# A first layer's weights finished by an accumulating DMA, and one output of the first token pair by seven products

## The chip, the cores and the metric

The kernel runs on one core of one Trainium2 chip. The metric is device microseconds (us) of one execution, the median over runs; a profile of one further execution gives the trace. PE is TensorE (matmuls), PEld its weight loads, DVE is VectorE, ACT is ScalarE, POOL is GpSimd and SP is SyncE, which here only issues DMAs.

## The reference

An attention over 256 channels, then two feed-forward layers of 2048 hidden columns, on 6016 tokens. The weights come in as float64.

```
qn = q / (norm(q, axis=1) + 1e-6);  kn = k / (norm(k, axis=1) + 1e-6)
a = softmax(kn.T @ qn / tau)              # 256 x 256, summed over 6016 tokens
x = v @ a                                 # 6016 x 256
h = x @ w_in;  g = h * sigmoid(1.702 * h) # 2048 columns
x = g @ w_out
h = x @ w_in2; g = max(h, 0) + alpha * min(h, 0)
out = g @ w_out2
```

## The kernel before, in words

**Numbers.** Every operand is kept as two float32r halves, hi and lo, and a product is three matmuls: hi by hi, hi by lo, lo by hi (`PASSES`). A matmul of the bulk is 128x128 weights by 512 tokens.

**Stages.** First q and k stream in and PE builds the 256 x 256 matrix of their products (gram, L348); ACT and DVE build the norms; a softmax follows (L457 to L480). The attention matrix is multiplied into the first layer's inner weights, so that v goes straight into the feed-forward layer: `emit_w(j)` (L483) makes the inner weights of output block j, `emit_pair(j)` (L628) of two blocks at once. Then come twelve token columns in six pairs, for layer 0 and then for layer 1; j counts eight blocks (`NQ`) of 256 hidden columns.

**The first pair.** For layer 0 the first pair of columns is run by `direct` while its weights are still being made. One unit of `direct` is one half block by one column: two products into one PSUM bank (L684), with the output products of the block before (`outs.next()`, L713) between them, 12 matmuls in all. Then, for the unit, ACT writes g (L761) and its hi half (L775), `mid_way` may emit weights, `beside(FIRST)` fills in background work, and DVE writes the lo half (L781). There are four units to a block, i = 0 to 3. All other pairs are run by `quartet`, which needs seven products instead of eight for a block and column pair (sums of operands, `T1` to `T4`, and sums of weights, `combine_wi`, prepared by DVE and ACT).

**The converter.** Float64 weights are turned into hi and lo by `Convert`, a piece of 512 columns (or 1024) at a time. Its steps: `load` (SP, into the buffer `raw`), `scale` (ACT, L130), `shift` (DVE, L133), `signed` (DVE, L137), `copy` (ACT, L143, the hi half), `power` (DVE, L147), `rest` (DVE, L150), `less` (DVE, L166) and `low` (DVE, L169, the lo half). `conv.todo` is the list of pieces: ia[j] for inner, ob_[j] for outer weights. `Converter.step` does the next DVE step; ACT's parts go onto the list `put_off`, which `beside` empties first. `beside` also takes steps while its time allows, and `need` takes them until a piece is made. So the order on every engine is fixed when the program is built; each engine runs its own list in order, and waits on semaphores for the others. `raw` has two buffers, and `rest` is the last step that reads one: the next load waits for it.

Of the kernel before, what the change touches and what calls it, by code (L numbers as in the profile page):

```python
# [15 lines left out]
P = 128  # L16
N = 6016
C = 256
# [16 lines left out]
TAIL = 12  # L35
ON_VECTOR = (4, 5, 6, 8)
# [20 lines left out]
def attention_then_two_ffns(ctx: ExitStack, tc: tile.TileContext, q, k, vT, tau, w1i, w1o, w2i, w2o, alpha, outT):  # L57
# [45 lines left out]
    class Convert:  # L103
# [4 lines left out]
        most = 2 * PIECE  # L108
        pool = None

        def __init__(self, src, pair, done=None):
            self.src, self.pair, self.done = src, pair, done
            self.made = False
            self.a = src.shape[1]
            self.n = self.a * src.shape[2]
# [7 lines left out]
        def load(self):  # L123
            self.raw = self.tile("raw", U32, RAWS, 2)
            nc.sync.dma_start(self.raw.rearrange("p (a n) w -> p a (n w)", a=self.a), u32(self.src))

        def scale(self):

            self.p = self.tile("p", F32, 2)
            nc.scalar.activation(self.p, f32(self.raw[:, :, 1]), AF.Copy, scale=2.0**-112)  # L130
# [4 lines left out]
        def signed(self):  # L135
            self.top = self.tile("top", F32, 1)
            nc.vector.scalar_tensor_tensor(u32(self.top), self.raw[:, :, 1], 0x80000000, u32(self.p),  # L137
                                           ALU.bitwise_and, ALU.bitwise_or)
            self.hi, self.lo = self.pair()
            put_off.append(self.copy)  # L140

        def copy(self):
            nc.scalar.copy(self.hi, self.like(self.top))  # L143
# [30 lines left out]
    class Converter:  # L174


        STEPS = (("shift", 0.45), ("signed", 0.7), ("power", 0.45), ("rest", 0.7), ("less", 0.7), ("low", 0.7))

        def __init__(self):
            self.todo, self.loaded, self.ready, self.open, self.at = [], [], [], None, 0  # L180

            self.ahead = False
            self.held = 0

        def load(self):

            while self.todo and len(self.loaded) + len(self.ready) + self.held < RAWS:
                x = self.todo.pop(0)
                x.load()
                self.loaded.append(x)  # L190

        def scale(self):
            if self.loaded and not self.ready:
                x = self.loaded.pop(0)
                put_off.append(x.scale)
                self.ready.append(x)

        def cost(self):
            return self.time(self.open or (self.ready + self.loaded + self.todo)[0])

        def time(self, piece):
            t = self.STEPS[self.at][1]
            return 2 * t - 0.15 if piece.n > PIECE else t

        def waits(self):

            if not self.open:
                if not self.loaded and not self.ready:
                    self.load()
                self.scale()  # L210
            return any(x in put_off for x in self.needs())

        def needs(self):
            return [self.ready[0].scale] if self.at == 0 else [self.open.copy] if self.at == 4 else []

        def step(self):

            if self.waits():
                scalar_work()
            if not self.open:  # L220
                self.open = self.ready.pop(0)
                self.held = 1
            do, t = self.STEPS[self.at][0], self.time(self.open)
# [7 lines left out]
            if self.at == len(self.STEPS):  # L231
                self.open, self.at = None, 0
            return t
# [5 lines left out]
        def need(self, pieces):  # L239
            while not all(x.made for x in pieces):  # L240
                self.step()

        def left(self):
            return self.todo + self.loaded + self.ready + [x for x in (self.open,) if x]
# [10 lines left out]
    with tc.manual_schedule():  # L255
# [15 lines left out]
        def inner(j, n=1):  # L271
            def pair():
                if j % 2 == 0:
                    t = wi_whole[j] = wi_first.pop() if wi_first else wi_tiles()
                    for i in range(2):
                        wi_pair[j + i] = tuple(x[:, :, i * C:(i + 1) * C] for x in t)
                    if n == 2:
                        return [flat(x) for x in t]
                return wi_pair[j]
            return Convert(w1i.rearrange("p (a n) -> p a n", a=2)[:, :, j * C:(j + n) * C], pair)  # L280

        def outer(j, n=1):
            def pair():
                return tuple(WO[:, j:j + n, h].rearrange("p q a b -> p q (a b)") if n > 1 else flat(WO[:, j, h]) for h in range(2))
            return Convert(w1o[:, j * PIECE:(j + n) * PIECE].rearrange("p (a n) -> p a n", a=1), pair)

        ia, ob_ = {}, {}
        for made, piece, spans in ((ia, inner, ((0, 1), (1, 1), (2, 1), (3, 1), (4, 2), (6, 2))),
                                   (ob_, outer, ((0, 1), (1, 1), (2, 1), (3, 1), (4, 2), (6, 2)))):
# [254 lines left out]
        def prepare(l, p):  # L544
# [4 lines left out]
            ops = operands[l, p] = {}  # L549
# [40 lines left out]
            ]  # L590
            return early, late
# [63 lines left out]
        def beside(time, convert=False, place=None, most=None):  # L655

            now = scalar_work(most)
# [19 lines left out]
        def finish(steps):  # L677

            while any(s in bg for s in steps):
                bg.pop(0).run()  # L680
# [102 lines left out]
        def direct(j, outs, mid_way):  # L783

            ops = operands[0, 0]
            units = []
            for i, (f, c) in enumerate((f, c) for f in range(2) for c in range(2)):
                ps = begun.pop(0) if begun else None
                for h in range(2):
                    if h == 0 and ps:  # L790
                        continue
                    ps = ps or psh.tile([P, T], F32, tag="h", name="ps_h")
                    product(ps, j, 2 * h + f, ops[h, c], T, h == 0, h == 1)
                    outs and outs.next()
                u = Unit(0, 2 * j + f, c)
                u.take(ps)
                u.act()
                u.high()
                mid_way(i)
                beside(FIRST, convert=True)  # L800
                u.low()
                units.append((f, c, u.pair))
            return Outs(0, 0, j, units)

        def quartet(l, p, j, outs, carry):
# [3 lines left out]
            late = steps_late if j == 0 else []  # L809

# [3 lines left out]
            def copy(ps):  # L814
                s = sp.tile([P, T], F32, tag="s", name="s", bufs=3)
# [5 lines left out]
            most = 1 if l else None  # L821
# [105 lines left out]
        del raws[0, 0], raws[0, 1]  # L927
        outs = None
        steps_late = []
        combined = []  # L930
        for j in range(NQ):
# [3 lines left out]
            def mid_way(i):  # L935
                if j == 0 and i == 1:
                    conv.need([ob_[0]])
                    emit_w(1)
                if j in (1, 2, 3, 5) and i == 1:
                    (emit_w if j < 3 else emit_pair)(j + 1)  # L940
                if j == 2 and i == 0:
                    nc.sync.dma_start(alpha_sb, alpha)
                if j == 3 and i < 2:
                    load_tokens(0, 2 + i)
                if j == 5 and i == 0:
                    early, late = prepare(0, 1)
                    bg.extend(early + late)
                    for n in range(AHEAD):
                        combined.append(combine_wi(n))
                        bg.extend(combined[n])  # L950

            outs = direct(j, outs, mid_way)
        conv.need(ob_.values())
        finish(list(bg))
# [4 lines left out]
        stage = stx.enter_context(tc.tile_pool(name="stage", bufs=3, side="right"))  # L959
        Convert.pool, Convert.most = stx.enter_context(tc.tile_pool(name="cn", bufs=1, side="right")), PIECE  # L960
# [40 lines left out]
        carry = []  # L1001
        order = [(0, p) for p in range(1, NP)] + [(1, p) for p in range(NP)]
        for i, (l, p) in enumerate(order):
# [6 lines left out]
            for j in range(NQ):  # L1010
# [18 lines left out]
                if i == 0 and j + AHEAD < NQ:  # L1029
                    combined.append(combine_wi(j + AHEAD))  # L1030
                    first(combined[-1])
# [12 lines left out]
                if i == 0 and j + 1 < NQ:  # L1044
# [56 lines left out]
```

## Time and profile before

| | |
|---|---|
| median of 3 runs | 1034.63 us (1034.33 to 1034.76) |
| the profiled execution | 1034.38 us |
| its span, first to last instruction | 1032.6 us |
| PE busy | 1027.4 us (99%), 4640 matmul records |
| DVE busy | 765.3 us (74%) |
| ACT busy | 752.8 us (73%) |
| POOL busy | 31.3 us (3%) |

The busy shares are averages over the whole span. A matmul record of the bulk lasts 385 ns, but matmuls are pipelined and overlap, so the time that one adds is read from the starts of a run of them. Idle time before an instruction stands in brackets in a timeline, with what ended it.

### The profile page before, as it was taken

What the parts mean: (1) busy time and instruction counts of PE and PEld (TensorE: products, weight loads), DVE (VectorE), ACT (ScalarE), POOL (GpSimd) and SP (SyncE); (2) the same over time, 40 slices, a digit from 0 to 9 for tenths busy, and PEclk for the clock granted to TensorE, in tenths of its full rate; (3) what the DMA queues carried; (4) which work ended last, traced back from release to release, by engine and by line L of the source; (5) the groups of instructions that cost most, each with busy time, mean ns of one, the idle gap of its engine ahead of it and who ended that gap; (6) DMA issues with size and microseconds to landing.
All of it is one profiled execution on the core that took longest, in us unless ns stands there. A gap on an engine that the chain in (4) does not pass through costs nothing.

```text
span 1032.6 us, 12486 instructions
## 1 busy us (share of the span) xinstructions
PE 1027.4 (99%) x4640; PEld 866.8 (84%) x4640; DVE 765.3 (74%) x1230; ACT 752.8 (73%) x1255; POOL 31.3 (3%) x42
## 2 busy tenths in 40 slices
PE   9999999999999999999999999999999999999998
PEld 8888888888888888888998888888888888888997
DVE  4889967878778787445637777787877787877766
ACT  6777767778777777666767777777777777867776
POOL 4400000000000000000100000000000000000000
PEclk9999999999999999999999999999999999999999
DMA  9635102125224323003543001001001000000101
GB/s 361 240 106 180 42 23 95 42 77 179 77 82 158 101 93 133 1 1 126 200 169 113 1 21 62 1 21 62 1 21 62 1 18 25 35 0 1 42 1 36
DMA packets 30461, 77.62 MB, mean 75 GB/s; under 512 B 3008, under 2 KB 7616, under 8 KB 30144
## 3 DMA queue, kind: packets, MB, share of 16 engines
q1 hardware_dynamic: 28096, 65.29, 18.2%
q0 software_dynamic: 2304, 11.54, 3.4%
q8 instruction: 36, 0.59, 0.2%
q14 instruction: 25, 0.20, 0.1%
HBM read 52.96 MB, written 23.86 MB: 74 GB/s over the span
## 4 chain that ended last, share of the span: by engine, by line
PE 99%; DMA 0%; SPq 0%; ACT 0%; issue 0%
PE ps_o L713 50%; PE ps_h L684 44%; PE gram L348 4%; PE pw L483 1%; PE pw L628 1%; DMA qk<-in_k 0%; SPq L368 0%; PE nrm L426 0%; ACT s L730 0%; PE bc L448 0%; PE pt L471 0%
## 5 line engine op out<-in xcount | busy, mean ns | idle before, releaser
L713 PE MATMUL ps_o<-ghi,wo 128*128 128x512 f32 (+1 forms) x1536 | 561.6, 385 | 0.0
L684 PE MATMUL ps_h<-x,wi 128*128 128x512 f32 (+1 forms) x2040 | 550.5, 385 | 0.0
L684 PEld LDWEIGHTS ps_h<-x,wi 128*128 128x128 f32 x2040 | 382.2, 188 | 72.4 <-DVE wi L495 0.4
L713 PEld LDWEIGHTS ps_o<-ghi,wo 128*128 128x128 f32 x1536 | 288.3, 188 | 53.5
L713 PE MATMUL ps_o<-glo,wo 128*128 128x512 f32 (+1 forms) x768 | 296.0, 385 | 0.0
L750 DVE TENSOR_TENSOR g<-ps_h,s 128x512 f32<-128x512 f32 (+1 forms) x177 | 120.0, 678 | 94.1 <-PE ps_h L684 60.4
L779 DVE SCALAR_TENSOR_TENSOR glo<-g,sign_sb,ghi 128x512 fp32r<-128x512 f32 (+1 forms) x192 | 141.4, 736 | 55.5 <-ACT ghi L773 51.1
L816 ACT COPY s<-ps_h 128x512 f32<-128x512 f32 (+1 forms) x177 | 102.2, 577 | 104.7 <-PE ps_h L684 100.4
L781 DVE TENSOR_TENSOR glo<-g,ghi 128x512 fp32r<-128x512 f32 (+1 forms) x192 | 126.4, 677 | 68.1 <-ACT ghi L775 67.9
L713 PEld LDWEIGHTS ps_o<-glo,wo 128*128 128x128 f32 x768 | 144.2, 188 | 27.3 <-DVE glo L779 0.3
L773 ACT ACTIVATE ghi<-g,sign_sb 128x512 fp32r<-128x512 f32 (+1 forms) x192 | 137.0, 714 | 16.1 <-DVE g L769 10.8
L775 ACT CAST ghi<-g 128x512 fp32r<-128x512 f32 (+1 forms) x192 | 113.3, 612 | 3.6
L761 ACT ACTIVATE g<-ps_h 128x512 f32<-128x512 f32 (+1 forms) x112 | 65.7, 587 | 44.6 <-PE ps_h L684 43.9
L765 ACT ACTIVATE g<-g,sign_sb 128x512 f32<-128x512 f32 (+1 forms) x97 | 69.5, 717 | 29.2 <-DVE g L750 28.6
L769 DVE SCALAR_TENSOR_TENSOR g<-g,slope_sb 128x512 f32<-128x512 f32 (+1 forms) x97 | 71.6, 738 | 16.8 <-ACT g L765 16.6
L769 DVE SCALAR_TENSOR_TENSOR g<-ps_h,slope_sb,g 128x512 f32<-128x512 f32 (+1 forms) x95 | 69.7, 733 | 0.0
L827 ACT COPY ps_h<-ps_h 128x512 f32<-128x512 f32 (+1 forms) x87 | 49.0, 563 | 28.2 <-PE ps_h L684 27.6
L765 ACT ACTIVATE g<-ps_h,sign_sb 128x512 f32<-128x512 f32 (+1 forms) x95 | 64.3, 676 | 2.2 <-ACT g L765 0.3
L761 ACT ACTIVATE g<-g 128x512 f32<-128x512 f32 (+1 forms) x80 | 49.8, 623 | 15.5 <-DVE g L750 15.3
L348 PE MATMUL gram<-qk 128*128 128x256 f32 x156 | 34.3, 380 | 0.3 <-DMA qk<-in_k 0.3
L348 PEld LDWEIGHTS gram<-qk 128*128 128x128 f32 x156 | 29.4, 190 | 4.6 <-issue 0.7
L563 DVE TENSOR_TENSOR x<-t,x 128x512 fp32r<-128x512 f32 (+1 forms) x44 | 29.0, 671 | 0.0
(115 smaller groups left out, 498.6 us busy)
## 6 DMA issues: line engine op xcount, KB each, us to landing
wi<-w2i POOLq DMA_DIRECT2D x8, 896.0 KB, 4.9
xraw<-in_vT SPq DMA_DIRECT2D x10, 512.0 KB, 6.1
x<-ob SPq DMA_DIRECT2D x20, 256.0 KB, 2.3
xraw<-x SPq DMA_DIRECT2D x10, 512.0 KB, 3.5
out_T<-ob SPq DMA_DIRECT2D x20, 256.0 KB, 2.1
qk<-in_q SPq DMA_DIRECT2D x9, 512.0 KB, 10.2
qk<-in_k SPq DMA_DIRECT2D x9, 512.0 KB, 10.3
raw<-in_w2i SPq DMA_DIRECT2D x8, 512.0 KB, 4.2
```

The costliest lines, as they stand in the source:

```text
L348: nc.tensor.matmul(gram[m][:, :C], tiles[i][:, 1, r, m * P:(m + 1) * P], tiles[i][:, 0, r, :], start=(t == 0), stop=(t == R - 1))
L684: nc.tensor.matmul(ps[:, :n], WI[:, wq, a, blk], x[:, b, :n], start=(start and i == 0), stop=(stop and i == 2), skip_group_check=True)
L713: nc.tensor.matmul(acc_ps[c][d][:, :n], WO[:, j, a, f, d * P:(d + 1) * P], (hi, lo)[b][:, :n], start=(start and i == 0), stop=(stop and i ...
L750: nc.vector.tensor_tensor(self.src, ps[:, :self.n], s[:, :self.n], ALU.add)
L761: nc.scalar.activation(self.g, self.src, AF.Gelu_apprx_sigmoid)
L765: nc.scalar.activation(self.g, self.src, AF.Copy, scale=sign_sb[:, self.f])
L769: nc.vector.scalar_tensor_tensor(self.g, self.src, slope_sb[:, self.f], self.g, ALU.mult, ALU.max)
L773: nc.scalar.activation(self.hi, self.g, AF.Copy, scale=sign_sb[:, self.f])
L775: nc.scalar.copy(self.hi, self.g)
L779: nc.vector.scalar_tensor_tensor(self.lo, self.g, sign_sb[:, self.f], f32(self.hi), ALU.mult, ALU.subtract)
L781: nc.vector.tensor_tensor(self.lo, self.g, f32(self.hi), ALU.subtract)
L816: nc.scalar.copy(s[:, :n], ps[:, :n])
```

## The change

1. **An accumulating DMA.** Pieces ia[3] to ia[7] and ob_[2] to ob_[7] are `added`: after `rest`, POOL issues a DMA that adds `top` onto `p` (`sent`), ACT copies `p` to the hi half, and one DVE subtraction (`split`) gives the lo half; `less` and `low` go. All pieces are 512 wide now; there are three `raw` buffers, five of `p` and three of `top`.
2. **Given out by places.** Each call of `beside` is a place (`conv.place`). A piece's `scale` is put off until `LOADING` = 2 places after its load was issued, its copy until `LANDING` = 3 places after the DMA was issued, unless `need` asks for it.
3. **Seven products.** Block 7 of the first pair goes through `quartet`; its operand sums are prepared from block 4 on, the weight sums of block 7 from block 5 on.
4. **Buffers.** Five of the eleven token buffers lie in the lower pool instead of four.

```
+LOADING = 2
+LANDING = 3
+STRASSEN = 7
...
-            self.raw = self.tile("raw", U32, RAWS, 2)
+            self.begun = conv.now
+            self.raw = self.tile("raw", U32, Convert.raws, 2)
...
+        def sent(self):
+            self.begun = conv.now
+            nc.gpsimd.dma_start(out=self.p, in_=self.top, accum_op=ALU.add)
+
+        def split(self):
+            nc.vector.tensor_tensor(self.lo, self.like(self.p), f32(self.hi), ALU.subtract)
+            self.made = True
...
+        ADDED = (("shift", 0.45), ("signed", 0.7), ("power", 0.45), ("rest", 0.7))
...
-        def scale(self):
-            if self.loaded and not self.ready:
+        def scale(self, force=False):
+            while self.loaded and not self.ready and (force or not (self.ahead and Convert.deep) or self.now - self.loaded[0].begun >= LOADING):
                 x = self.loaded.pop(0)
                 put_off.append(x.scale)
                 self.ready.append(x)
...
+        def ask(self):
+            if self.flying and not self.flying[0].asked:
+                self.flying[0].asked = True
+                put_off.append(self.flying[0].copy)
...
+        def place(self):
+            self.now += 1
+            if self.ahead and Convert.deep:
+                self.scale()
+                if self.flying and self.now - self.flying[0].begun >= LANDING:
+                    self.ask()
...
-        conv.todo = [ia[1], ob_[0], ia[2], ob_[1], ia[3], ob_[2], ia[4], ob_[3], ob_[4], ia[6], ob_[6]]
+        conv.todo = [ia[1], ob_[0], ia[2], ob_[1], ia[3], ob_[2], ia[4], ia[5], ob_[3], ob_[4], ia[6], ia[7], ob_[5], ob_[6], ob_[7]]
...
-            return xin[i > 3].tile([P, 2, T], F32R, tag=f"x{i}", name="x")
+            if slot[0] <= 8:
+                i = (2, 1, 4, 0, 3, 5, 6, 7)[i]
+            return xin[i > 4].tile([P, 2, T], F32R, tag=f"x{i}", name="x")
...
         def beside(time, convert=False, place=None, most=None):
 
+            conv.place()
             now = scalar_work(most)
...
+                if j == 4 and i == 0:
+                    sums0.extend(prepare(0, 0))
+                    bg.extend(sums0)
...
+            if j < STRASSEN:
+                outs = direct(j, outs, mid_way)
+                continue
...
+            outs = quartet(0, 0, j, outs, carry)
```

The change moves instructions on ACT and DVE around `emit_w(3)`, which PE runs right after unit i = 1 of block 2. On ACT, before, from unit i = 1 of block 1 to unit i = 3; wi_hi_563<-top_626 is the hi half of ia[3], `p<-raw` a `scale`:

```order
L761 ACTIVATE g_647<-ps_h_630 128x512
L775 CAST ghi_645<-g_647 128x512
L491 ACTIVATE wi_436<-pw_650,rs_127 128x256 x2
L143 CAST wi_hi_563<-top_626 128x2x256
L761 ACTIVATE g_689<-ps_h_674 128x512
L775 CAST ghi_687<-g_689 128x512
L130 ACTIVATE p_692<-raw_598 128x512
L761 ACTIVATE g_714<-ps_h_699 128x512
L775 CAST ghi_712<-g_714 128x512
```

With the change, from the two weight rows of that piece (L571, before L491) to the copy of ia[3] behind unit i = 0 of block 2; p_599 is the sum of ia[3], raw_572 holds ob_[2], raw_603 ia[4], raw_673 ia[5] and raw_702 ob_[3]:

```order
L571 ACTIVATE wi_438<-pw_653,rs_127 128x256 x2
L137 ACTIVATE p_670<-raw_572 128x512
L848 ACTIVATE g_695<-ps_h_680 128x512
L862 CAST ghi_693<-g_695 128x512
L137 ACTIVATE p_698<-raw_603 128x512
L848 ACTIVATE g_724<-ps_h_709 128x512
L862 CAST ghi_722<-g_724 128x512
L137 ACTIVATE p_727<-raw_673 128x512
L848 ACTIVATE g_751<-ps_h_736 128x512
L862 CAST ghi_749<-g_751 128x512
L137 ACTIVATE p_755<-raw_702 128x512
L154 CAST wi_hi_568<-p_599 128x2x256
```

The hi half of ia[3] moved from before unit i = 2 of block 1 to behind unit i = 0 of block 2, and behind the scales of ob_[2], ia[4], ia[5] and ob_[3].

On DVE, before, from `rest` of ia[3] to `rest` of ob_[2]; the third row is the lo half of ia[3]:

```order
L150 SCALAR_TENSOR_TENSOR p_622<-raw_567,p_622 128x512
L166 TENSOR_TENSOR top_626<-top_626,wi_hi_563 128x512
L169 TENSOR_TENSOR wi_lo_564<-top_626,p_622 128x2x256
L781 TENSOR_TENSOR glo_646<-g_647,ghi_645 128x512
L133 TENSOR_SCALAR p_692<-p_692 128x512
L137 SCALAR_TENSOR_TENSOR top_695<-raw_598,p_692 128x512
L147 TENSOR_SCALAR p_692<-top_695 128x512
L781 TENSOR_TENSOR glo_688<-g_689,ghi_687 128x512
L150 SCALAR_TENSOR_TENSOR p_692<-raw_598,p_692 128x512
```

With the change, from `signed` of ob_[2] on (`rest` of ia[3] and `shift` of ob_[2] stand right ahead of it) to the lo half of ia[3], the last row:

```order
L144 SCALAR_TENSOR_TENSOR top_677<-raw_572,p_670 128x512
L868 TENSOR_TENSOR glo_649<-g_650,ghi_648 128x512
L158 TENSOR_SCALAR p_670<-top_677 128x512
L161 SCALAR_TENSOR_TENSOR p_670<-raw_572,p_670 128x512
L140 TENSOR_SCALAR p_698<-p_698 128x512
L144 SCALAR_TENSOR_TENSOR top_706<-raw_603,p_698 128x512
L868 TENSOR_TENSOR glo_694<-g_695,ghi_693 128x512
L158 TENSOR_SCALAR p_698<-top_706 128x512
L161 SCALAR_TENSOR_TENSOR p_698<-raw_603,p_698 128x512
L140 TENSOR_SCALAR p_727<-p_727 128x512
L868 TENSOR_TENSOR glo_723<-g_724,ghi_722 128x512
L168 TENSOR_TENSOR wi_lo_569<-p_599,wi_hi_568 128x2x256
```

The lo half of ia[3] moved behind the four steps of ob_[2], the four of ia[4] and the first of ia[5]. Ahead of `rest` of ia[3] DVE's list is as before back to the gram's end.

On SP, in the change, the loads from ia[4] to ob_[4], behind which alpha's follows:

```order
L132 DMA raw_603<-in_w1i 128x2x512
L132 DMA raw_673<-in_w1i 128x2x512
L132 DMA raw_702<-in_w1o 128x1024
L132 DMA raw_731<-in_w1o 128x1024
L1048 DMA alpha_sb_69<-in_alpha 128x16
```

The load of ia[5] (raw_673) takes the buffer that `rest` of ia[3] frees, that of ob_[3] (raw_702) the one that `rest` of ob_[2] frees. In the first loads behind q and k, ob_[0] now stands ahead of the two loads of tokens, and ia[2] ahead of tau.

## Rows read from the trace of the kernel before

**Rows 1.** The page, parts 1, 2 and 4: busy time, clock in 40 slices, chain.
```profile
PE 1027.4 (99%) x4640; PEld 866.8 (84%) x4640; DVE 765.3 (74%) x1230; ACT 752.8 (73%) x1255; POOL 31.3 (3%) x42
...
PEclk9999999999999999999999999999999999999999
...
PE 99%; DMA 0%; SPq 0%; ACT 0%; issue 0%
```

**Rows 2.** Waits of PE over the whole span: total us, times, longest.
```profile
PE idle L308 <- POOL ones L301: 1.1, 1, 1.1
PE gram L348 <- DMA qk<-in_k: 0.3, 1, 0.3
```

**Rows 3.** The chain in order of time: start, us, what.
```profile
147.13 1.36 PE ps_o L713 x6
```

**Rows 4.** Stretches: length, then busy us of PE, PEld, DVE, ACT, POOL; clock, DMA, GB/s.
```profile
77.10:91.00 13.90, 13.90 (x63) 11.49 (x62) 13.12 (x19) 10.11 (x18) 0.00 (x0) 1.00 0.37 115
...
133.50:146.50 13.00, 13.00 (x59) 10.75 (x58) 7.00 (x16) 6.74 (x12) 0.00 (x0) 1.00 0.00 1
```

**Rows 5.** Timeline of PE at `emit_w(3)`: start, us, what.
```profile
75.42 0.40 PE L483 MATMUL pw<-wi_hi,eT_hi 128*128 128x256 f32 x2
75.66 0.40 PE L483 MATMUL pw<-wi_lo,eT_hi 128*128 128x256 f32 x2
```

**Rows 6.** Timeline of DVE, from `rest` of ia[3] on.
```profile
70.39 0.68 DVE L150 SCALAR_TENSOR_TENSOR p<-raw,p 128x512 f32<-128x512 uint32 x1
71.00 0.68 DVE L166 TENSOR_TENSOR top<-top,wi_hi 128x512 f32<-128x512 f32 x1
71.71 0.69 DVE L169 TENSOR_TENSOR wi_lo<-top,p 128x512 fp32r<-128x512 f32 x1
...
72.92 0.42 DVE L133 TENSOR_SCALAR p<-p 128x512 uint32<-128x512 uint32 x1
...
75.05 0.68 DVE L150 SCALAR_TENSOR_TENSOR p<-raw,p 128x512 f32<-128x512 uint32 x1
```

**Rows 7.** Timeline of SP: issues of tau and of a load of weights.
```profile
35.32 0.34 SPq L417 DMA_DIRECT2D tau_sb<-in_tau  x1
...
71.15 0.55 SPq L125 DMA_DIRECT2D raw<-in_w1i  x1
```

**Rows 8.** DMA issues from 60 to 72 us: count, KB each, us to landing.
```profile
raw<-in_w1i SPq DMA_DIRECT2D x1, 512.0 KB, 4.0
raw<-in_w1o SPq DMA_DIRECT2D x1, 512.0 KB, 3.5
```

**Rows 9.** Timeline of ACT around the same place.
```profile
65.17 0.66 ACT L130 ACTIVATE p<-raw 128x512 f32<-128x512 f32 x1
65.74 0.59 ACT L761 ACTIVATE g<-ps_h 128x512 f32<-128x512 f32 x1
...
66.89 0.47 ACT L491 ACTIVATE wi<-pw,rs 128x256 fp32r<-128x256 f32 x1
...
69.86 0.61 ACT L143 CAST wi_hi<-top 128x512 fp32r<-128x512 f32 x1
...
76.47 1.15 ACT L130 ACTIVATE p<-raw 128x1024 f32<-128x1024 f32 x1 [0.59 <-DMA raw<-in_w1i]
```

**Rows 10.** DMA issues of line L1037, POOL's loads of weights of 896 KB each.
```profile
DMA to landing us min/median/max: 4.7/4.9/6.8
```

**Rows 11.** Timeline of ACT at the end of the gram.
```profile
39.44 0.62 ACT L325 CAST x<-xraw 128x512 fp32r<-128x512 f32 x1
41.79 0.37 ACT L429 COPY G<-gram 128x256 f32<-128x256 f32 x1 [1.74 <-PE gram L348]
```

**Rows 12.** DMA issues from 32 to 42 us.
```profile
GB/s 385 369 385 393 385 393 381 381 373 348 352 340 373 389 389 377 385 385 385 369 410 385 402 393 393 393 402 418 410 410 401 320 165 66 66 17 33 16 0 0
...
tau_sb<-in_tau SPq DMA_DIRECT2D x1, 0.5 KB, 6.9
```

**Rows 13.** Timeline of DVE at its first use of tau.
```profile
43.86 0.13 DVE L441 RECIPROCAL tau_sb<-tau_sb 128x1 f32<-128x1 f32 x1
```

More of the change, by code (lines that the diff above doesn't have):

```diff
@@ L103, in attention_then_two_ffns, with __init__ @@
     class Convert:
-        most = 2 * PIECE
+        most = PIECE
         pool = None
-        def __init__(self, src, pair, done=None):
-            self.src, self.pair, self.done = src, pair, done
+        deep = True
+        raws = 3
+        def __init__(self, src, pair, done=None, added=False):
+            self.src, self.pair, self.done, self.added = src, pair, done, added
+            self.asked = False
             self.made = False
@@ L185, in load @@
         def load(self):
-            while self.todo and len(self.loaded) + len(self.ready) + self.held < RAWS:
+            while self.todo and len(self.loaded) + len(self.ready) + self.held < Convert.raws:
                 x = self.todo.pop(0)
@@ L196, in scale, with next, list, landed @@
                 self.ready.append(x)
+        def next(self):
+            return self.open or (self.ready + self.loaded + self.todo + [None])[0]
+        def list(self, piece):
+            return self.ADDED if piece and piece.added else self.STEPS
         def cost(self):
-            return self.time(self.open or (self.ready + self.loaded + self.todo)[0])
+            return self.time(self.next())
         def time(self, piece):
-            t = self.STEPS[self.at][1]
-            return 2 * t - 0.15 if piece.n > PIECE else t
+            if not piece:
+                return 0.7
+            if self.landed():
+                return 0.7
+            return self.list(piece)[self.at][1]
+        def landed(self):
+            return self.flying and self.flying[0].asked and self.flying[0].copy not in put_off
+        def ask(self):
+            if self.flying and not self.flying[0].asked:
+                self.flying[0].asked = True
+                put_off.append(self.flying[0].copy)
         def waits(self):
+            if not self.next():
+                return not self.landed()
+            if self.landed():
+                return False
             if not self.open:
@@ L210, in waits, with settle @@
                 self.scale()
+                if not self.ready:
+                    return True
             return any(x in put_off for x in self.needs())
         def needs(self):
-            return [self.ready[0].scale] if self.at == 0 else [self.open.copy] if self.at == 4 else []
+            if not self.next() or self.landed():
+                return []
+            if self.at == 0:
+                return [self.ready[0].scale]
+            if self.open.added:
+                return []
+            return [self.open.copy] if self.at == 4 else []
+        def settle(self):
+            self.flying.pop(0).split()
         def step(self):
             if self.waits():
+                if not self.open:
+                    self.scale(True)
                 scalar_work()
+            if not self.next() or self.landed():
+                self.settle()
+                return 0.7
             if not self.open:
@@ L222, in step @@
                 self.held = 1
-            do, t = self.STEPS[self.at][0], self.time(self.open)
+            steps = self.list(self.open)
+            do, t = steps[self.at][0], self.time(self.open)
             getattr(self.open, do)()
@@ L230, in step @@
                     self.load()
-            if self.at == len(self.STEPS):
+            if self.at == len(steps):
+                if self.open.added:
+                    self.open.sent()
+                    self.flying.append(self.open)
                 self.open, self.at = None, 0
@@ L239, in need @@
         def need(self, pieces):
-            while not all(x.made for x in pieces):
-                self.step()
+            for x in pieces:
+                while not x.made:
+                    if x not in self.flying:
+                        self.step()
+                        continue
+                    self.ask()
+                    if self.flying[0].copy in put_off:
+                        put_off.remove(self.flying[0].copy)
+                        self.flying[0].copy()
+                    self.settle()
+        def place(self):
[3 more added lines that the diff above has]
+                if self.flying and self.now - self.flying[0].begun >= LANDING:
+                    self.ask()
         def left(self):
-            return self.todo + self.loaded + self.ready + [x for x in (self.open,) if x]
+            return self.todo + self.loaded + self.ready + [x for x in (self.open,) if x] + self.flying
     conv = Converter()
@@ L284, in pair @@
                 return tuple(WO[:, j:j + n, h].rearrange("p q a b -> p q (a b)") if n > 1 else flat(WO[:, j, h]) for h in range(2))
-            return Convert(w1o[:, j * PIECE:(j + n) * PIECE].rearrange("p (a n) -> p a n", a=1), pair)
+            return Convert(w1o[:, j * PIECE:(j + n) * PIECE].rearrange("p (a n) -> p a n", a=1), pair, added=j > 1)
         ia, ob_ = {}, {}
-        for made, piece, spans in ((ia, inner, ((0, 1), (1, 1), (2, 1), (3, 1), (4, 2), (6, 2))),
-                                   (ob_, outer, ((0, 1), (1, 1), (2, 1), (3, 1), (4, 2), (6, 2)))):
+        for made, piece, spans in ((ia, inner, [(j, 1) for j in range(NQ)]),
+                                   (ob_, outer, [(j, 1) for j in range(NQ)])):
             for j, n in spans:
@@ L590, in prepare @@
             ]
+            if (l, p) == (0, 0):
+                return [early[i] for i in (2, 3, 6, 7)] + [late[i] for i in (0, 1, 2, 4, 5)]
             return early, late
@@ L679, in finish @@
             while any(s in bg for s in steps):
-                bg.pop(0).run()
+                s = bg.pop(0)
+                if s.waits():
+                    put_off.remove(s.needs)
+                    s.needs()
+                s.run()
         def product(ps, wq, blk, x, n, start, stop):
@@ L799, in direct @@
                 mid_way(i)
-                beside(FIRST, convert=True)
+                beside(FIRST, convert=not own_first[0], most=2 if (j, i) == (STRASSEN - 1, 3) else None)
                 u.low()
@@ L820, in quartet @@
             ends = (l, p, j) == (1, NP - 1, NQ - 1)
-            most = 1 if l else None
+            most = 1 if l else 2 if narrow else None
             u11, u22, u21, u12 = (Unit(l, 2 * j + f, c) for f, c in ((0, c0), (1, c1), (1, c0), (0, c1)))
@@ L935, in mid_way @@
             def mid_way(i):
[L936 to L940, printed above, removed]
+                if j < 3 and i == 1:
+                    if j == 0:
+                        conv.need([ob_[0]])
+                    emit_w(j + 1)
+                if j == 3 and i == 1:
+                    emit_pair(4)
+                if j == 5 and i == 1:
+                    emit_pair(6)
+                    own_first[0] = True
+                    combining_of(7)
                 if j == 2 and i == 0:
                     nc.sync.dma_start(alpha_sb, alpha)
[L943 to L952, printed above, removed]
+                if j == 4 and i == 0:
+                    sums0.extend(prepare(0, 0))
+                    bg.extend(sums0)
+                if j == 6 and i == 0:
+                    own_first[0] = False
+                    finish(sums0)
+                    for c in range(2):
+                        load_tokens(0, 2 + c)
+                    combining_of(0)
+                if j == 6 and i == 2:
+                    pair1.extend(prepare(0, 1))
+                    bg.extend(pair1[0])
+            if j < STRASSEN:
+                outs = direct(j, outs, mid_way)
+                continue
+            finish(combined[j])
+            rest = [x for x in pair1[0] if x in bg]
+            for x in rest:
+                bg.remove(x)
+            first(rest + pair1[1])
+            outs = quartet(0, 0, j, outs, carry)
         conv.need(ob_.values())
-        finish(list(bg))
+        finish(combined[0] + pair1[0])
+        steps_late = [x for x in pair1[1] if x in bg]
         smx.close()
@@ L1028, in attention_then_two_ffns @@
                     first(rest + nxt_late)
-                if i == 0 and j + AHEAD < NQ:
-                    combined.append(combine_wi(j + AHEAD))
-                    first(combined[-1])
+                if i == 0:
+                    fresh = [n for n in ((1, 2) if j == 0 else (j + 2,)) if n < STRASSEN]
+                    combined.update({n: combine_wi(n) for n in fresh})
+                    first(sum((combined[n] for n in fresh), []))
                 outs = quartet(l, p, j, outs, carry)
```

42 lines of the change are left out of this document (30 added, 12 removed).

## The prediction

> **What bounds the kernel now.** I read the page first: PE is busy for 1027.4 of 1032.6 us, the chain that ended last is 99% PE, and the clock stands at 9 in every slice, which is the upper of TensorE's two levels, 2.4 GHz [rows 1]. "Busy" alone does not show that PE is fed, so the waits of PE come next: two in the whole span, 1.1 us for the first constants and 0.3 us for the first of q and k [rows 2]. Then the price of a matmul: six of them take 1.36 us on the chain, 0.227 us each [rows 3], not the 385 ns that one record lasts. So PE is the bound from end to end. Little can be won except by fewer matmuls, and whatever makes PE wait shows one to one, since no later slack takes it up. Last I read DVE and ACT in the stage that the change rewrites: DVE is busy for 13.12 of 13.90 us while pieces are converted, and for 7.00 of 13.00 us when the last weights are done [rows 4]. DVE is nearly full where the conversion is rearranged and half idle where the seven products come in.
>
> **The products.** Block 7 of the first pair loses one product of eight: three matmuls of 512 columns, 3 x 0.227 = **-0.68 us**. PE's list in the built program is shorter by these three, so the change does what it says, and that is all of PE's saving. The operand sums for it (five differences and four lo halves at 0.69 us on DVE [rows 6], some 6 us) fall into blocks 4 to 6, and the conversion gives back 0.69 us of DVE for every 512 columns that are added by DMA (two DVE steps out, one in; eleven pieces, 7.6 us) but loses the cheaper double-width steps. DVE's load is about level there, with the idle half of block 7 behind it: I take 0. If that cover were gone, one lo half late for PE would cost 0.69 us.
>
> **The early loads.** SP now issues the load of ob_[0] ahead of the tokens and that of ia[2] ahead of tau, each 512 KB. At some 390 GB/s [rows 12] that makes tokens and tau 1.3 us late. The first copy of tokens began at 39.44 and lasts 0.62 us; it would end at 41.4, and ACT idles until 41.79 behind it [rows 11]. Tau was issued at 35.32 [rows 7] and took 6.9 us [rows 12], so it lands at 42.2, then at 43.5; DVE first reads it at 43.86 [rows 13]. Both fit, by 0.3 to 0.4 us: 0, at most 0.5. The fifth buffer in the lower pool and the other numbering change no instruction's length: 0.
>
> **The wait that I expect.** PE runs `emit_w(3)` at 75.42 and needs the hi half of ia[3] there, the lo half at 75.66 [rows 5]. Before, ACT made the hi half at 69.86 [rows 9] and DVE ended the lo half at 71.71 + 0.69 = 72.40 [rows 6], over 3 us early. Now both stand behind other work. Step by step, with DVE's list unchanged up to `rest` of ia[3], which ends at 70.39 + 0.68 = 71.07 [rows 6]:
> - That frees a buffer, and the load of ia[5] is issued, as a load was there before, at 71.15 [rows 7].
> - DVE goes on with ob_[2] at 71.00: shift, signed, power and rest, with one lo half of g among them. The same five took from 72.92 to 75.05 + 0.68, that is 2.81 us, in the trace [rows 6]. So `rest` of ob_[2] ends at 73.8.
> - Only then can ob_[3] be loaded, into the buffer that this frees: issued at 73.9 and, at the 3.5 us that such a load took [rows 8], landed at **77.4**.
> - On ACT the load of ia[5] has landed at 71.15 + 4.0 = 75.15 [rows 8]; its scale and g and hi of the next unit take 1.72 us (65.17 to 66.89, [rows 9]), to 76.9. Then comes the scale of ob_[3], which waits for 77.4, and behind it in the queue stands the copy of ia[3], though its data are long there. Scale to next start is 0.57 us and the copy lasts 0.61 [rows 9]: the hi half is ready at 77.4 + 0.57 + 0.61 = 78.6.
> - PE wanted it at 75.42 and waits **3.2 us**. Two matmuls later (75.66 - 75.42 = 0.24) it wants the lo half, which DVE can write only from the hi half on, in 0.69 us [rows 6]: another 0.69 - 0.24 = **0.45 us**.
>
> The place count does not prevent this: it counts calls in program order, two units of 2.72 us for a load, but DVE's `rest` that frees the buffer runs far behind its unit, since DVE is the engine that is behind here. That ACT does stand waiting for such a load the trace shows once, at 76.47, for 0.59 us [rows 9].
>
> The load of ob_[3] is not alone: the accumulating DMA of ob_[2] starts at the same moment and moves 256 KB, 0.7 us at 390 GB/s [rows 12], or 1.3 if each byte counts twice. Between 0 and 1.3 I take 0.35, nearer the row without sharing because the load was issued first. So the stall is 3.65 to 5.0 us, and I take **4.0**.
>
> After it PE is 4 us later, while DVE, which was behind, stood still for less; both engines are then closer to PE than before, and the next weights, wanted by `emit_pair(4)` more than four units on, have that much more slack. I count nothing there.
>
> **The accumulating DMA itself** has no row. It is off the path as long as it lands before its copy on ACT can run: for ia[3], sent at 71.1 and copied at 78.0, 6.9 us. The loads that POOL issued, 896 KB each, landed in 4.7 to 6.8 us [rows 10]; a quarter of the bytes, read twice and written once, should land sooner, and I take it as in time. From below the cost is 0; from above, twice the middle row, 9.8 us, which would land 2.9 us late.
>
> **Sum.** 4.0 - 0.68 = +3.3 us on the profiled execution's 1034.38, so 1037.7; the median is 0.25 above that execution, so **1037.9** in runs. Its own range is 1037.1 (a stall of 3.65 us less some tenths) to 1039.3 (5.0 us). A measurement of this kernel can tell some 0.2%, 2.07 us, from no change.
>
> **Rivals.**
> *No stall, only the products.* Against my sum: if `rest` of ob_[2] ended by 70.6 instead of 73.8, the load would be there in time and PE would save 0.68 us: 1033.9, not slower. It decides at DVE's lag, and the lag is read from rows ahead of any changed instruction on DVE; what could shorten it is an ACT queue rid of copies earlier on (DVE waited there for weights, not for copies). I give it 0.17, and 0.03 to more than 0.2% faster, for which no row offers the 2 us.
> *Late accumulation.* If each accumulating DMA takes 9.8 us, the copy of ia[3] starts at 80.9 and PE waits 2.9 us more, and where `need` asks for an outer piece at a block's start PE may wait again: 1040.8 for one wait. For it speaks that POOL writes the DMA's entries while DVE is busy for 94% of the time [rows 4]; against it, 896 KB landed in 4.9 us [rows 10]. The Trainium skill ("SBUF — State Buffer", SBUF: two separate sides) states a rule against this change: a DMA issued by GpSimd waits for its descriptors while VectorE runs an operation that takes both ports, and it gives 3.1 us beside such work where 0.62 us was needed alone. By that rule, as an estimate, 2.5 us come on top of each transfer, which would put the 4.9 us row at 7.4 and the copy half a microsecond late; no run here shows it yet. Chance 0.10.
> *The clock falls.* If the gap lets TensorE fall to 1.2 GHz, each place of 12 matmuls run at that level costs its 2.72 us again: 1040.6 for one place. In the trace the clock stays at the upper level throughout, with no gap over 1.1 us [rows 1, 2], so neither side is shown. The Trainium skill ("TensorE: Matmul & The Clock Gate", HAM oscillation — how this bites in real kernels) says that long gaps in PE's work do throttle the clock. Chance 0.05.
>
> **Numbers.** One stall and nothing else 0.65, late accumulation 0.10, clock 0.05: slower by over 0.2% 0.80. The same 0.17, faster 0.03. The range runs from the case without a stall, 1033.9, to 1041.0, which takes in one late accumulation or one slow place; above lie repeated ones.
>
> **What would show it.** Right: PE idle some 3 to 4 us at `emit_w(3)`, ended by ACT's cast of wi_hi, then about 0.5 us ended by DVE; ACT idle before it until the load of ob_[3]; no other wait of PE; three matmuls fewer in block 7. Wrong: PE without a wait there, a wait of ACT's cast for POOL's DMA, a second gap at `emit_pair` or at the start of a block, or a clock below the upper level.

## The result, and the profile after

The changed kernel takes **1040.71 us** (median of 6 runs, 1039.8 to 1042.62), beside 1034.52 us (1034.28 to 1034.76) for the kernel before on the same chip: ratio 1.0063, 95% interval 1.005 to 1.0076. It is slower by 6.2 us, where 3.3 us were forecast (1037.9); the time lies inside the stated range, near its upper end. The profiled execution took 1040.91 us, its span is 1039.1 us.

The page of the kernel after, parts 1, 2 and 4, answers to [rows 1]:

```profile
PE 1029.5 (99%) x4637; PEld 868.3 (84%) x4637; DVE 767.6 (74%) x1254; ACT 757.9 (73%) x1270; POOL 41.0 (4%) x53
...
PEclk9998999999999999999999999999999999999999
...
PE 97%; DVE 1%; ACT 1%; DMA 1%; issue 0%; POOL 0%; SPq 0%; DVEq 0%; POOLq 0%
```

PE has three records fewer, so the product is gone; yet the chain holds some DVE, ACT and DMA now, and in one slice, the fourth, the clock is below 9. All the waits of PE, as in [rows 2]:

```profile
PE pw L563 <- ACT wi_hi L154: 5.0, 1, 5.0
PE idle L386 <- POOL ones L379: 1.1, 1, 1.1
```

There is one new wait in this list, at `emit_w(3)` (L563 is L483 before), and no other to the end of the program; a second, short one at the same place comes below. The timeline of PE there (start, us, what, idle before and what ended it), to be laid beside [rows 5]:

```profile
75.20 0.39 PE L800 MATMUL ps_o<-ghi,wo 128*128 128x512 f32 x1
80.58 0.80 PE L563 MATMUL pw<-wi_hi,eT_hi 128*128 128x256 f32 x2 [4.99 <-ACT wi_hi L154]
81.31 0.80 PE L563 MATMUL pw<-wi_lo,eT_hi 128*128 128x256 f32 x2
...
83.61 0.63 PE L771 MATMUL ps_h<-x,wi 128*128 128x512 f32 x1
```

`emit_w(3)` starts at 80.58 instead of 75.42: 5.16 us late. What held it is read on four queues. DVE, as in [rows 6], from `rest` of ia[3] on:

```profile
70.44 0.68 DVE L161 SCALAR_TENSOR_TENSOR p<-raw,p 128x512 f32<-128x512 uint32 x1
...
73.16 0.69 DVE L161 SCALAR_TENSOR_TENSOR p<-raw,p 128x512 f32<-128x512 uint32 x1
...
80.56 0.69 DVE L168 TENSOR_TENSOR wi_lo<-p,wi_hi 128x512 fp32r<-128x512 f32 x1 [3.01 <-ACT wi_hi L154]
```

SP, as in [rows 7]:

```profile
71.19 0.55 SPq L132 DMA_DIRECT2D raw<-in_w1i  x1
73.92 3.06 SPq L132 DMA_DIRECT2D raw<-in_w1o  x2
```

The DMAs issued between 73 and 75 us (count, KB each, us to landing), as in [rows 8]:

```profile
raw<-in_w1o SPq DMA_DIRECT2D x1, 512.0 KB, 5.4
p<-top POOLq DMA_DIRECT2D x1, 256.0 KB, 6.3
```

And ACT, as in [rows 9]:

```profile
75.83 0.67 ACT L137 ACTIVATE p<-raw 128x512 f32<-128x512 f32 x1 [2.40 <-DMA raw<-in_w1i]
76.40 0.57 ACT L848 ACTIVATE g<-ps_h 128x512 f32<-128x512 f32 x1
77.01 0.62 ACT L862 CAST ghi<-g 128x512 fp32r<-128x512 f32 x1
79.36 0.66 ACT L137 ACTIVATE p<-raw 128x512 f32<-128x512 f32 x1 [1.74 <-DMA raw<-in_w1o]
79.92 0.60 ACT L154 CAST wi_hi<-p 128x512 fp32r<-128x512 f32 x1
```

Read them in order: `rest` of ob_[2] ends at 73.85 and frees the buffer; the load of ob_[3] is issued at 73.92 and lands 5.4 us later; ACT stands for its scale until 79.36; only then, at 79.92, comes the copy of ia[3]. Its own DMA had landed 2.8 us before, at 77.1. POOL's timeline has its issue, and the DMAs issued between 71 and 72 us its 5.6 us to landing:

```profile
71.46 1.03 POOL L165 DMA_DIRECT2D p<-top  x1 [31.59 <-DVE p L140]
...
p<-top POOLq DMA_DIRECT2D x1, 256.0 KB, 5.6
```

Behind the wait the clock is down. Stretches of 1 us (length; busy us of PE, PEld, DVE, ACT, POOL; granted clock, DMA share, GB/s), as in [rows 4]:

```profile
77.00:78.00 1.00, 0.00 (x0) 0.00 (x0) 0.55 (x1) 0.62 (x1) 0.73 (x1) 1.00 0.96 262
78.00:79.00 1.00, 0.00 (x0) 0.00 (x0) 0.00 (x0) 0.00 (x0) 0.00 (x0) 0.59 1.12 279
...
84.00:85.00 1.00, 1.00 (x4) 0.77 (x3) 0.48 (x1) 0.45 (x2) 0.28 (x1) 0.50 0.60 68
85.00:86.00 1.00, 1.00 (x6) 0.82 (x5) 0.59 (x2) 0.86 (x2) 0.00 (x0) 0.99 0.67 176
```

PE had stood still from 75.6; the granted clock falls in the stretch from 78 us, is 0.50, which is 1.2 GHz, until 85 us, and then is back at 2.4. The same work took longer than before. The first and second group of products behind `emit_w(3)`, before:

```profile
76.86 0.85 PE L684 MATMUL ps_h<-x,wi 128*128 128x512 f32 x3
...
78.24 0.84 PE L684 MATMUL ps_h<-x,wi 128*128 128x512 f32 x3
```

And after, from the third pair of matmuls of `emit_w(3)` on:

```profile
81.91 0.63 PE L563 MATMUL pw<-wi_hi,eT_lo 128*128 128x256 f32 x2
...
85.65 0.86 PE L771 MATMUL ps_h<-x,wi 128*128 128x512 f32 x3
```

`emit_w(3)` took 83.61 - 80.58 = 3.03 us against 76.86 - 75.42 = 1.44, and the next group of products 2.04 against 1.38, together 2.25 us more. Not all of that is the clock. DVE ended the lo half at 80.56 + 0.69 = 81.25, and PE began on it at 81.31, 0.06 us later, as it had begun on the hi half 0.06 us after ACT's cast ended (79.92 + 0.60 = 80.52). So PE waited for the lo half as well; the wait stands with PE's weight loads:

```profile
81.31 0.50 PEld L563 LDWEIGHTS pw<-wi_lo,eT_hi 128*128 128x128 f32 x2 [0.22 <-DVE wi_lo L168]
```

The four pairs of matmuls behind it take 83.61 - 81.91 = 1.70 us, and six at that pace would take 2.55. So 3.03 - 2.55 = 0.48 us is the late lo half, with PE's restart behind it, and 2.25 - 0.48 = 1.77 us the clock. The account: 5.16 + 0.48 + 1.77 - 0.68 = 6.73 us. The last matmul, before and after, starts 6.77 us later:

```profile
1028.42 0.37 PE L713 MATMUL ps_o<-ghi,wo 128*128 128x448 f32 x1
...
1035.19 0.37 PE L800 MATMUL ps_o<-ghi,wo 128*128 128x448 f32 x1
```

So less than 0.1 us is lost or won in the rest of the program.

### The profile page after: what moved, and what is told of

Its sections match the earlier page's. It is cut to its first block, busy times and chain, and to the rows that moved or that the text cites. A ratio compares the mean times of both kernels' runs of the same rounds, so it can differ in the third digit from the quotient of the medians.

```text
span 1039.1 us, 12565 instructions
## 1 busy us (share of the span) xinstructions
PE 1029.5 (99%) x4637; PEld 868.3 (84%) x4637; DVE 767.6 (74%) x1254; ACT 757.9 (73%) x1270; POOL 41.0 (4%) x53
## 4 chain that ended last, share of the span: by engine, by line
PE 97%; DVE 1%; ACT 1%; DMA 1%; issue 0%; POOL 0%; SPq 0%; DVEq 0%; POOLq 0%
PE ps_o L800 49%; PE ps_h L771 43%; PE gram L428 4%; PE pw L563 1%; PE pw L710 1%; DMA raw<-in_w1o 1%; PE idle L386 0%; DVE top L144 0%; DVE glo L868 0%; DVE p L161 0%; DVE p L158 0%; ACT g L848 0%; ACT wi L571 0%; ACT L1014 0%; DVE top L185 0%
## 5 line engine op out<-in xcount | busy, mean ns | idle before, releaser
L643 DVE TENSOR_TENSOR x<-t,x 128x512 fp32r<-128x512 f32 (+1 forms) x48 | 31.5, 672 | 0.0
```

## The experiments

Each is an edit of the changed kernel, timed beside the kernel before, with a profile.

| run | what | median us | ratio, 95% interval | longest wait of PE behind the gram | clock after it in the profile |
|---|---|---|---|---|---|
| after | the change | 1040.71 | 1.0063, 1.005 to 1.0076 | 5.0 | 0.50 |
| e1_late_pieces | late pieces alone added | 1033.48 | 0.9992, 0.9983 to 1.0 | none | 1.00 |
| e2_no_sum | accumulating DMA left out | 1039.0 | 1.0044, 1.003 to 1.0058 | 3.6 | 0.50 |
| e3_copy_first | copy ahead of scale | 1038.21 | 1.0034, 1.0022 to 1.0046 | 2.5 | 0.50 |
| e4_dma_alone | eight products | 1041.88 | 1.0077, 1.0062 to 1.0093 | 5.6 | 0.50 |
| e5_late_eight | e1 with eight products | 1034.22 | 0.9998, 0.9988 to 1.0008 | none | 1.00 |
| e6_ia3_plain | ia[3] not added | 1037.0 | 1.0026, 1.0016 to 1.0036 | 1.2 | 1.00 |
| e7_no_adding | no piece added | 1042.41 | 1.0079, 1.0064 to 1.0094 | 3.5 | 0.50 |
| e8_copy_first_later | e3, scales a place later | 1036.98 | 1.0027, 1.0016 to 1.0039 | 2.1 | 0.50 |

The profile is of one run. The mean granted clock of the other runs tells whether it fell there too: it did in every run of after, e2, e4 and e7 (0.996 to 0.998), in four of five of e3 and three of six of e8 (0.998, the others 1.000), in one of eight of e6 (0.998, the others 0.999 and more), and in none of e1 and e5 (0.999 and more).

### Which pieces are added

```
-            return Convert(w1i...[:, :, j * C:(j + n) * C], pair, added=j > 2)
+            return Convert(w1i...[:, :, j * C:(j + n) * C], pair, added=j > 5)
...
-            return Convert(w1o[:, j * PIECE:(j + n) * PIECE]..., pair, added=j > 1)
+            return Convert(w1o[:, j * PIECE:(j + n) * PIECE]..., pair, added=j > 3)
```

> The changed kernel with only the later pieces (inner 6 and 7, outer 4 to 7) finished by the accumulating DMA; inner 3 to 5 and outer 2 and 3 go by the old six steps, all 512 wide. Theory A (the wait is the copy of inner piece 3 in ACT's queue, made late by the new order of the first added pieces): no wait of PE at emit_w(3), the clock stays at its upper level, and only the three matmuls count: 1034.5 - 0.7 = 1033.8 us. Rival B (accumulating DMAs hurt wherever they stand, by their landing or by what they do to the loads): waits reappear at the later pieces, over 1036 us. Rival C (the seven products cost PE something themselves): a wait of PE after 130 us, and no gain over before.

Measured: 1033.48 us (1033.08 to 1034.48, 11 runs) beside 1034.4 (1034.18 to 1034.93, 16 runs). All the waits of PE:

```profile
PE idle L386 <- POOL ones L379: 1.1, 1, 1.1
PE gram L428 <- DMA qk<-in_k: 0.7, 2, 0.4
```

So the loss of 7.2 us against this run lies wholly in giving ia[3] to ia[5] and ob_[2], ob_[3] to the DMA, while DVE is behind; the later six pieces can go that way at no cost. It is the fastest kernel of the study, though its interval just reaches 1.

> Edit: in the changed kernel only ia[3] goes back to the six steps without the accumulating DMA; ob_[2], ob_[3] and ia[4] on keep it. Theory A (DVE is behind in blocks 1 to 4, so every piece whose sum comes late there makes PE wait at the point that needs it): no wait at emit_w(3), whose hi half is no longer behind the scale of ob_[3], but waits at the next points of need, the first use of ob_[2] at about 85 us and emit_pair(4) at about 92 us, of 1 to 3 us each and some with the clock down behind them: 1035.5 to 1039 us. Theory B (the only fault is the queue of ACT at emit_w(3)): no wait at all, 1033.5 us as e1_late_pieces.

Edit: `added=j > 3` for the inner weights, `j > 1` kept for the outer ones. Measured: 1037.0 us. Waits of PE behind the gram:

```profile
PE ps_o L800 <- ACT wo L154: 1.2, 1, 1.2
...
PE pw L710 <- ACT wi_hi L154: 0.7, 1, 0.7
PE pw L710 <- DVE wi_lo L168: 0.6, 1, 0.6
...
PE ps_o L800 <- DVE wo L168: 0.2, 1, 0.2
```

They lie at 84.04 us, the first use of ob_[2], and at 90.31, `emit_pair(4)`: with one piece taken out, the next ones come late where they are needed. So the fault is not one slot of ACT's queue: pieces behind ia[3] that are added while DVE is behind come late too. The waits sum to 2.7 us and the kernel is 3.5 us above e1, with the clock of the profiled run at its upper level throughout. The listed waits are too short, since each is counted from the modelled end of the matmul before. By the starts of the same matmuls in e1's trace PE loses 3.9 us at the four, some 0.3 us more at each than is listed, and it had come there 0.6 us earlier than in e1.

### Queue, load or DMA

```
         def sent(self):
             self.begun = conv.now
-            nc.gpsimd.dma_start(out=self.p, in_=self.top, accum_op=ALU.add)
+            pass
```

> The changed kernel without the eleven accumulating DMAs: top is never added onto p, so the weights of those pieces lack their upper half; every other instruction and its order stay. Theory A: the queue order alone gives the wait. The load of outer piece 3 has the DMA engines to itself and lands in 3.5 instead of 5.4 us, so ACT's copy ends near 78.6 instead of 80.5 and PE waits 3.2 us in place of 5.0 at emit_w(3); 1034.5 - 0.7 + 3.2 + 0.5 = 1037.5 us if the clock stays up, up to 1039.7 if it falls as in the changed kernel (2.2 us). Rival B (the copy is late because the accumulation lands late): without it there is no wait, 1033.8 us.

The weights of those pieces then lack what the DMA would have added. Measured: 1039.0 us. The timeline of ACT:

```profile
78.05 0.66 ACT L137 ACTIVATE p<-raw 128x512 f32<-128x512 f32 x1 [0.83 <-DMA raw<-in_w1o]
78.61 0.60 ACT L154 CAST wi_hi<-p 128x512 fp32r<-128x512 f32 x1
```

The load of ob_[3], issued at 73.97, landed in 4.1 us instead of 5.4. PE still waits 3.6 us for the hi half and 0.2 for the lo half, and the clock still falls. So the order of the queues alone makes the wait; the accumulating DMAs lengthen it by 1.3 us, most likely by sharing the DMA engines. Their busy share from 77 to 78 us was 0.96 in the changed kernel; here, in the same columns, it is 0.63:

```profile
77.00:78.00 1.00, 0.00 (x0) 0.00 (x0) 0.56 (x1) 0.23 (x1) 0.00 (x0) 1.00 0.63 94
```

```
             if self.ahead and Convert.deep:
-                self.scale()
                 if self.flying and self.now - self.flying[0].begun >= LANDING:
                     self.ask()
+                self.scale()
```

> The changed kernel with two lines swapped: at a place the copy of a landed piece is asked for ahead of the next scale, so on ACT the copy of inner piece 3 stands before the scale of outer piece 3, still behind that of inner piece 5. Theory A: the copy no longer waits for the load of outer piece 3 (79.34) and starts when ACT is through with the unit, near 77.6; hi half at 78.2, PE waits 2.8 instead of 5.0 us and then 0.45 for the lo half; a gap this short should leave the clock up: 1034.5 - 0.7 + 3.3 = 1037.1 us. Rival B (the landing of the sum is the wait): the copy still starts near 79.9, and the time stays at 1040.7 us.

Measured: 1038.21 us. With the copy ahead of the scale of ob_[3] the wait is 2.5 us, half of 5.0: ACT's order was worth that much. The part on the clock was wrong in four of the five runs, the profiled one among them:

```profile
80.00:81.00 1.00, 1.00 (x7) 1.00 (x6) 0.97 (x3) 0.76 (x2) 0.00 (x0) 0.50 1.05 311
```

The fifth, at a mean granted clock of 1.000, took 1036.77 us, near the 1037.1 of theory A; the four took 1037.87 to 1038.53.

> Edit: as e3_copy_first (at each place the copy is put on ACT's list ahead of the next scale), and a scale is put off until three places after its load instead of two (LOADING = 3), so that ACT does not stand behind a load just issued. Theory A (what is left of the wait in e3, 2.5 us, is ACT standing for the load of ia[5] and then the accumulating DMA's landing at about 77.1 us): PE waits 1.5 to 2.2 us at emit_w(3) for the copy, and TensorE's clock, which fell behind a wait of 2.5 us in e3, stays at 2.4 GHz: 1035.5 us (1035.0 to 1036.2). Theory B (the clock falls behind this wait too): the same wait and 1.1 to 1.7 us more, 1036.9 us. Theory C (the later scales make DVE late elsewhere): further waits of PE, above 1037.5 us.

Edit: as e3, with `LOADING = 3`. Measured: 1036.98 us in the median of six runs. The timeline of ACT in the profiled one, which took 1037.7:

```profile
76.99 0.62 ACT L154 CAST wi_hi<-p 128x512 fp32r<-128x512 f32 x1 [2.50 <-DMA p<-top]
```

That of PE:

```profile
77.67 0.80 PE L563 MATMUL pw<-wi_hi,eT_hi 128*128 128x256 f32 x2 [2.14 <-ACT wi_hi L154]
```

And stretches of 1 us behind it, in the columns used above:

```profile
79.00:80.00 1.00, 1.00 (x6) 1.00 (x6) 0.93 (x3) 0.33 (x1) 0.00 (x0) 0.50 1.09 310
80.00:81.00 1.00, 1.00 (x6) 1.00 (x5) 1.00 (x2) 0.07 (x1) 0.05 (x1) 0.50 1.05 277
81.00:82.00 1.00, 1.00 (x5) 0.77 (x5) 0.67 (x2) 0.45 (x2) 0.83 (x1) 0.95 0.79 152
```

Here ACT stands for the accumulating DMA itself, and nothing else is ahead of the copy: its landing is the next bound, 2.1 us after PE wants the weights. This short wait of PE was followed by the lower clock in the profiled run, but not in every run: three took 1037.47 to 1038.27 us at a mean granted clock of 0.998, three 1036.22 to 1036.48 at 1.000. So theory B holds for one half of the runs, and theory A, just above its range, for the other. The median lies between two groups, and that it agrees with theory B's 1036.9 is chance. With the clock up the kernel is 2.7 to 3.0 us above e1, about the wait for the two halves; the fall costs some 1.5 us more, as theory B has it. A fourth `raw` buffer, which would let the load of ob_[3] start earlier, was not tried.

### The seven products

```
-STRASSEN = 7
+STRASSEN = 8
...
-                    own_first[0] = True
-                    combining_of(7)
+                if j == 3 and i < 2:
+                    load_tokens(0, 2 + i)
+                if j == 5 and i == 0:
+                    early, late = prepare(0, 1)
+                    bg.extend(early + late)
...
```

> The changed kernel with block 7 of the first pair by eight products again and the plan of before for that pair's background work; the converter and its accumulating DMAs as changed. Theory A: the same wait at emit_w(3) and the same fall of the clock, and three matmuls more: 1040.7 + 0.7 = 1041.4 us. Rival C (the seven products or the operand sums prepared for them cause part of the loss): clearly under 1040 us.

Measured: 1041.88 us, PE waiting 5.6 us at `emit_w(3)`; the load of ob_[3] took 6.0 us there. The loss is the conversion's, without the seven products too.

> Edit: in the changed kernel only ia[6], ia[7] and ob_[4] to ob_[7] are given to the accumulating DMA (as in e1_late_pieces), and block 7 of the first pair keeps its eight products (as in e4_dma_alone). Theory A (the two parts of the change are independent: the products are worth three matmuls, 0.68 us, and a conversion that makes PE wait nowhere is worth nothing): e1 plus 0.7, that is 1034.2 us (1033.9 to 1034.6), PE with no wait behind the gram, level with the kernel before. Theory B (the gain of e1 comes from the conversion, and the products cost in DVE work what they save): 1033.5 us, as e1.

Edit: e1 and e4 together. Measured: 1034.22 us, theory A: 0.74 us above e1, where three matmuls are 0.68 us, and level with the kernel before (1034.32 beside it). So all of the gain in e1 is the products', and a conversion that PE never waits for is worth nothing by itself.

> Edit: in the changed kernel no piece is given to the accumulating DMA; the seven products, the three raw buffers, the 512-wide pieces and the new list of loads stay. Theory A (the accumulating DMA is worth something only as relief of DVE, and DVE has no room for the pieces of blocks 4 to 7 together with the operand sums of the seven products): no wait at emit_w(3), but PE waits late, around the start of block 7 at 130 to 155 us, for 3 to 6 us in all: 1036.5 to 1039.5 us. Theory B (DVE has the room, the adding is worth nothing): 1033.5 us, as e1_late_pieces.

Edit: `added` dropped for all pieces. Measured: 1042.41 us; the place was as in theory A, and so was the sum of the waits, 5.8 us of 3 to 6; the time is 3 us above its range, which left out the fall of the clock. Waits of PE:

```profile
PE ps_h L771 <- ACT wi L695: 4.7, 2, 3.5
PE ps_h L771 <- DVE wi L692: 1.1, 1, 1.1
```

The timeline of ACT ahead of the longest:

```profile
149.27 0.62 ACT L695 CAST wi<-s 128x512 fp32r<-128x512 f32 x1 [2.78 <-DVE s L689]
```

No wait at `emit_w(3)`, but waits at 134.5, 136.4 and 150 us for sums of weights that DVE made too late, and a clock of 0.50 from 149 to 155 us. Here the accumulating DMA earns its keep: seven products need the DVE time that it frees in the later pieces.

## Why the prediction was right and wrong

- **The products, -0.68 us**: right; e5 less e1 is 0.74 us, or 0.82 when each is taken against the kernel before beside it (-0.10 and -0.92). That their operand sums cost nothing, because the conversion gives DVE time back, was right as well, and e7 shows that it hung on that.
- **The early loads, 0**: right; `rest` of ia[3] begins at 70.44 against 70.39 [rows 6], with no new wait ahead of it.
- **Place and mechanism of the wait**: right, step by step: `rest` of ob_[2] ended at 73.85 (73.8 forecast), the load was issued at 73.92 (73.9), and the copy stood in ACT's queue behind the scale that waits for it.
- **The load of ob_[3]**, the first of the two steps that failed: 3.5 us plus 0.35 for sharing was taken, "nearer the row without sharing because the load was issued first", and it took 5.4. Without the sums it took 4.1 (e2), so sharing with them cost 1.3 us, the upper end of the bound; being issued 0.25 us ahead of the sum of ob_[2], at 73.92 against 74.17, did not spare it that. That 1.3 us is just the bound is in part luck: the bound counted the sum of ob_[2] alone, and those of ia[3] (until 77.1) and ia[4] (from 76.87) overlapped the load too. The other 0.6 us over [rows 8] were there without the sums; in e2 the loads of ia[5] (until 75.39) and ob_[4] (from 76.69) overlapped this one, while that of [rows 8] had none beside it. No run separates them. The late hi half made PE start 5.16 us late instead of 3.2 + 0.35.
- **The lo half, 0.45 us**: right; 0.48 us in the account above, though PE's own rows list no wait for it.
- **The clock**, the second step that failed: it was put at nothing in the sum. The rival with the chance 0.05 came true beside the forecast and cost 1.77 us, less than its 2.72 us for one place, as most of the matmuls in the slow stretch are 256 columns wide. So the trace's miss, 6.73 us against 4.0 - 0.68 = 3.32, is 1.61 us of the hi half, 0.03 of the lo half and 1.77 of the clock. No row before showed a gap over 1.1 us, and the sum took the clock as given; a forecast wait of 4 us should have raised that question first. The stated range took in one slow place, and so the time lies in it; the sum's own range, to 1039.3, missed it. The Trainium skill ("TensorE: Matmul & The Clock Gate", HAM oscillation — how this bites in real kernels) says that long gaps throttle the clock. The runs agree for waits of 3.5 us and more, where the clock fell in every run; but 2.1 and 2.5 us, shorter than the gaps of that section, were followed by the fall too, in three of six and four of five runs (e8, e3).
- **Late accumulation** (0.10): not in the changed kernel, since the DMA of ia[3] landed at 77.1, ahead of the copy at 79.92. It is next in line: in e8 nothing but this DMA holds the copy. All eleven, in the group of that DMA in the kernel after:

```profile
DMA to landing us min/median/max: 3.3/5.3/6.5
```

  The rule from the Trainium skill ("SBUF — State Buffer", SBUF: two separate sides) by which I put such a transfer, as an estimate, at 7.4 us was not borne out in that size, and no run here separates its mechanism from the sharing of engines.
- **No stall** (1033.9 us): it needed the early pieces left alone; e1, which does so, gave 1033.48.

## What to carry to other kernels

A delay counted in program places protects nothing when the engine that frees the buffer runs behind its place: trace the freeing instruction in time, and look at what stands in the same queue behind the instruction that waits for the load. Move work off a full engine onto a slow path (a DMA with 5 us to landing) only for pieces that are needed much later than that. And price a forecast gap of PE as the gap plus the matmuls run at the lower clock behind it, as a risk even for a gap of 2 us; then read the clock of every run, since one profile and a median can hide that a kernel does both.

## What was not expected of the hardware

At `emit_w(3)` the clock fell behind waits of PE of 3.6, 5.0 and 5.6 us in every run, behind 2.5 us in four of five (e3) and behind 2.1 us in three of six (e8); it fell behind 3.5 us in every run of e7, and stayed up behind the 1.2 us and less in the profile of e6. Where one kernel ran both ways the fall cost some 1.5 us (e3, e8). An accumulating DMA of 256 KB from SBUF to SBUF took 3.3 to 6.5 us to land, 5.3 in the median, longer than the 4.1 us of a 512 KB load from HBM when that ran without such a DMA beside it.
